# Where the second mask product of a score stage stands among the score products

## The chip, the cores and the metric

The kernel runs on one core of a Trainium2 chip. The metric is device time in microseconds (us) of one execution; lower is better.

## The reference

Two independent parts read the same `x` of 2048 rows by 640 and are mixed by a gate `g` per row. Part B is a gated feed-forward layer. Part A is attention in 64 segments of 32 rows, with a memory of 8 rows that is carried from one segment to the next, so that the segments form a chain. All data are bfloat16.

```python
def _A_ref(x, mem0, Wq, Wk, Wv, Wo, seg_len):      # H = 32 heads, Dh = 192, M = 8, seg_len = 32
    idx = jnp.arange(M + seg_len)
    mask = (idx[:, None] < M) | (idx[:, None] >= idx[None, :])
    mem = mem0
    for s in range(n_seg):
        h = jnp.concatenate([mem, x[:, s * seg_len:(s + 1) * seg_len, :]], axis=1)
        q, k, v = (jnp.einsum('btd,dhe->bhte', h, W) for W in (Wq, Wk, Wv))
        scores = jnp.einsum('bhqe,bhke->bhqk', q, k) * scale
        scores = jnp.where(mask[None, None], scores, -1000000000.0)
        o = jnp.einsum('bhqk,bhke->bhqe', _softmax(scores), v)
        o = jnp.einsum('bhte,hed->btd', o, Wo)
        mem = o[:, :M, :]
        outs.append(o[:, M:, :])
    return jnp.concatenate(outs, axis=1)
...
return g * a + (1 - g) * b       # g = sigmoid(sum(x * gate_w)), a = part A, b = part B
```

## The kernel before, in words

Part B and the left columns of the first segments are worked out in the first stretch. Then `segment(s)` runs 64 times and issues its work in an order that is written out by hand: four lists, `PROG`, `PROG1`, `PROG` and `PROG3`, one for each `s % 4`. Each item of a list is one piece of work: `("g", group, k)` is a step of the projections Q, K and V (`proj`), `("tq", o)` and `("tk", o)` transpose the rows of Q and K (`row_transp`), `("sc", o)` makes the scores, `("ex", o)` the softmax, `("pt", o)` transposes the probabilities (`p_transp`), `("pv", o)` multiplies by V (`pv_oct`) and `("wo", ...)` projects out (`wo_part`, `wo_both`). The 32 heads go in four octets of eight, `o` from 0 to 3 (`NOCT` is 4).

TensorE's array is used in column tiles. The projections (L1138, L226, L930) and the output products (L1338, L1364) write 32 output rows each, four side by side; the probabilities' transposes (L1249, L1254) do so too. Scores and `pv_oct` (L1282, L1284) use two halves of 64 columns, at tile positions `(0, 0)` and `(0, 64)`, below called the lower and the upper half.

`scores(s, o)` fills one bank of PSUM with the scores of eight heads, four in each half, 40 by 40 each (`R` is 40: 32 rows and 8 of memory). The heads have 192 values, that is one and a half chunks of 128, so each head's score is one "outer" product over a whole chunk (L1195) and one "inner" product over half a chunk (L234 by `_matmul_rows` for the lower half; L1202 for the upper one, over a copy `Qz` of Q with zeros). Before them one product by the identity writes the mask into 4 x 40 columns of each half (L1187): with `start=True` it overwrites, and the score products add to it. The two masks are one operation of the scheduler, the sixteen score products are the next. Its inputs come from DVE (the transposes into `Qs` and `Ks`) and POOL (`Qz`, L1179, and the left columns, `left_fill`, L1012). After it DVE takes the row maximum (L1214).

The scheduler `_Sched` records operations, each a list of instructions on one engine, and derives from what they read and write which semaphores each must wait for. `finalize` drops waits that are already implied. `emit_stream` issues each remaining wait by `wait_ge` (L203) ahead of the operation's first instruction; where there is more than one, all but one become instructions of their own (EVENT_SEMAPHORE in the trace). For TensorE `finalize` first tries to hang waits on the last instructions of the operation in front:

```python
if E == "pe" and len(waits) > 1 and op.idx > 0:
    prev = self.streams["pe"][op.idx - 1]
    ...
    room = 0 if prev.name.startswith("ffn") else len(prev.fns) - 1 - len(prev.tail_waits)
    ...
        if room > 0 and sn.get("pe", -1) < prev.idx:
            moved.append(wv)
            room -= 1
        else:
            keep.append(wv)
```

Of the kernel before, what the change touches and what calls it, by code (L numbers as in the profile page):

```python
# [231 lines left out]
def _matmul_rows(e, out, lhsT, rhs, start, stop, tile_position):  # L232
    nm = e.bass.get_next_instruction_name()
    return e.add_instruction(mybir.InstMatmult(  # L234
        name=nm, start_tensor_calc=start, stop_tensor_calc=stop, tile_size=(128, 64), tile_position=tile_position,
        bass_skip_group_check=True, ins=[e.lower_ap(rhs), e.lower_ap(lhsT)], outs=[e.lower_ap(out)]))


def _build(nc, A_x, A_mem0, A_Wq, A_Wk, A_Wv, A_Wo, seg_len, w_gate, w_up, w_down,
# [13 lines left out]
    NOCT = NT // 4  # L253
# [4 lines left out]
    R = L + M  # L258
# [15 lines left out]
    S_ = _Sched(nc)  # L274
# [62 lines left out]
    ps = nc.alloc_psum_tensor("ps", [128, 8, 512], F32)  # L337
# [3 lines left out]
    o = wsA_base - wsB_total  # L341
# [6 lines left out]
    o = wsA_base  # L348
# [4 lines left out]
    o = ffn_base  # L353
# [66 lines left out]
    SC = 512 - 4 * R  # L420
# [37 lines left out]
    o = ffn_base - sum(fp_sz.values())  # L458
# [5 lines left out]
    gp = [fview(fp_off["gr"] + 4 * NSEG * i, 4 * NSEG) for i in range(4)]  # L464
# [38 lines left out]
    r_ps = [Rg("ps", b, b + 1) for b in range(8)]  # L503
# [96 lines left out]
    o = 0  # L600
# [73 lines left out]
    def load_residents(cls, pick=lambda key: True):  # L674
        for key in first:
# [7 lines left out]
           reads=[r_ident], writes=[r_ident])  # L683
# [10 lines left out]
    for i in range(2):  # L694
# [3 lines left out]
               reads=[r_elw], writes=[r_elw])  # L698
# [18 lines left out]
    for h in range(NH):  # L717
        for w_, sb_, rw_, nm in ((w_gate, wg_sb, r_wg, "wg"), (w_up, wu_sb, r_wu, "wu")):
            S_.add("sp", lambda e, h=h, w_=w_, sb_=sb_: e.dma_start(
                sb_[h], w_.rearrange("(p k) f -> p k f", p=128)[:, :, FH * h:FH * (h + 1)]),  # L720
                writes=[rw_[h]], dma_sem="%s%d" % (nm, h))
# [255 lines left out]
    for n, (g, o) in enumerate(units):  # L977
# [7 lines left out]
        if g == 0:  # L985
            S_.add("pool", lambda e, o=o, b=b: e.tensor_copy(out=stg[o // 2][:, o % 2], in_=lst[b][:, 0]), reads=[r_lst[b]], writes=[r_stgh[o // 2][o % 2]],
                   name="stg s0 o%d" % o)
# [22 lines left out]
    def left_fill(s, i):  # L1010
        o, h = octet(s, i), i // 2
        S_.add("pool", lambda e: e.tensor_copy(out=Qs[:, :, L:R], in_=stg[h][:, o % 2, 0]), reads=[r_stgh[h][o % 2]], writes=[r_Ql],  # L1012
               name="Ql s%d o%d" % (s, o))
        S_.add("pool", lambda e: e.tensor_copy(out=Ks[:, :, L:R], in_=stg[h][:, o % 2, 1]), reads=[r_stgh[h][o % 2]], writes=[r_Kl],
               name="Kl s%d o%d" % (s, o))
# [166 lines left out]

    def scores(s, o):
        bank = 5 + o % 2
        fns = []
        for gp in (0, 64):
            fns.append(lambda e, gp=gp: e.matmul(  # L1187
                ps[gp:gp + R, bank, SC:512].rearrange("p (t r) -> p t r", r=R),
                ident[:, 0:R], maskm.rearrange("p (o r) -> p o r", o=1).broadcast_to([128, 4, R]),
                start=True, stop=False, tile_position=(0, gp), skip_group_check=True))  # L1190
        S_.add("pe", fns, reads=[r_ident, r_maskm], writes=[r_ps[bank]], name="mask s%d o%d" % (s, o))
        fns = []
        for tl in range(4):
            for gp, c in ((0, 3 * tl), (64, 3 * tl + 2)):
                fns.append(lambda e, gp=gp, c=c, tl=tl: e.matmul(  # L1195
                    ps[gp:gp + R, bank, SC + tl * R:SC + (tl + 1) * R], Qs[:, c, :], Ks[:, c, :], start=False, stop=False,
                    tile_position=(0, gp), skip_group_check=True))
        for tl in range(4):
            c = 3 * tl + 1
            fns.append(lambda e, c=c, tl=tl: _matmul_rows(  # L1200
                e, ps[0:R, bank, SC + tl * R:SC + (tl + 1) * R], Qs[0:64, c, :], Ks[0:64, c, :], False, True, (0, 0)))
            fns.append(lambda e, c=c, tl=tl: e.matmul(  # L1202
                ps[64:64 + R, bank, SC + tl * R:SC + (tl + 1) * R], Qz[:, tl, :], Ks[:, c, :], start=False, stop=True,
                tile_position=(0, 64), skip_group_check=True))
        S_.add("pe", fns, reads=[r_Qm, r_Ql, r_Qz, r_Km, r_Kl], writes=[r_ps[bank]],
               name="sc s%d o%d" % (s, o))
        if o + 1 < NOCT:
            left_fill(s, o + 1)
        S3 = ps[0:104, bank, SC:512].rearrange("p (t r) -> p t r", r=R)
        mxs = st_f[o % 2][0][0:104, :]  # L1210
        rst = r_st[o % 2]
        mxb = mxs.rearrange("p (t o) -> p t o", o=1).broadcast_to([104, 4, R])
        rb = r_ps[bank]
        S_.add("dve", lambda e: e.tensor_reduce(out=mxs, in_=S3, axis=AX.X, op=ALU.max),  # L1214
               reads=[rb], writes=[rst], name="smax max")
        S_.add("dve", lambda e: e.tensor_tensor(out=S3, in0=S3, in1=mxb, op=ALU.subtract),  # L1216
               reads=[rb, rst], writes=[rb], name="smax sub")
# [244 lines left out]
    def segment(s):  # L1462
# [3 lines left out]
        for n, item in enumerate(PROGS[q]):  # L1466
# [12 lines left out]
            elif kind == "tk":  # L1479
                row_transp(s, 1, i)  # L1480
            elif kind == "sc":
                scores(s, i)
            elif kind == "ex":
                softmax(s, i)
# [192 lines left out]
```

## Time and profile before

| | |
|---|---|
| timed runs | 1657.43, 1655.54, 1647.93 us; median 1655.54 |
| span of the profiled execution | 2114.2 us; the page gives it no other time |
| granted TensorE clock in it | 0.654 |
| TensorE (PE) busy | 2098.0 us, 99% of the span |
| mask products, L1187 | 512, mean 247 ns |
| outer score products, L1195 | 2048, mean 180 ns |
| waits of their own on TensorE's loader, L203 | 54, median 51 ns |

The span is that of one execution under the profiler, at its granted clock; the timed runs are other executions. In the rows of the trace PE is a product, PEld the load of its weights, and the q of PEldq stands for the sequencer in front of an engine. Starts are us from the begin of the span. The duration of a product contains the depth of the pipe, so products overlap, and the pace is read from starts. A merged row shows the start of its first instruction and the end of its last.

### The profile page before, as it was taken

What the parts mean: (1) busy time and instruction counts of PE and PEld (TensorE: products, weight loads), DVE (VectorE), ACT (ScalarE), POOL (GpSimd) and SP (SyncE); (2) the same over time, 40 slices, a digit from 0 to 9 for tenths busy, and PEclk for the clock granted to TensorE, in tenths of its full rate; (3) what the DMA queues carried; (4) which work ended last, traced back from release to release, by engine and by line L of the source; (5) the groups of instructions that cost most, each with busy time, mean ns of one, the idle gap of its engine ahead of it and who ended that gap; (6) DMA issues with size and microseconds to landing.
All of it is one profiled execution on the core that took longest, in us unless ns stands there. A gap on an engine that the chain in (4) does not pass through costs nothing.

```text
span 2114.2 us, 75845 instructions
## 1 busy us (share of the span) xinstructions
PE 2098.0 (99%) x37107; PEld 958.1 (45%) x28147; DVE 1005.8 (48%) x3039; ACT 792.9 (38%) x1890; POOL 553.3 (26%) x1625
## 2 busy tenths in 40 slices
PE   9999999999999999999999999999999999999997
PEld 3444344444444444444444444444444444444444
DVE  4233254554545454545545454545455454545453
ACT  1111244343434343444434343434444343434342
POOL 1000023232232223232222323232322223222332
PEclk6666666666666666666666666666666666666666
DMA  9612577776768777677767677776777676777775
GB/s 319 182 33 57 184 268 260 248 270 232 253 219 275 244 258 241 227 255 254 274 233 249 221 268 249 255 251 225 248 256 270 239 258 212 261 256 249 254 264 174
DMA packets 275415, 499.28 MB, mean 236 GB/s; under 512 B 121119, under 2 KB 136327, under 8 KB 275079
## 3 DMA queue, kind: packets, MB, share of 16 engines
q1 hardware_dynamic: 271000, 491.30, 68.8%
q8 instruction: 255, 4.18, 0.8%
q10 hardware_dynamic: 4079, 3.14, 0.5%
q14 instruction: 81, 0.66, 0.1%
HBM read 473.25 MB, written 21.09 MB: 234 GB/s over the span
## 4 chain that ended last, share of the span: by engine, by line
PE 99%; DMA 0%; DVE 0%; SPq 0%; POOL 0%; ACT 0%; issue 0%; ACTq 0%; POOLq 0%; DVEq 0%
PE ps L226 26%; PE ps L1138 25%; PE ps L1338 9%; PE ps L1383 8%; PE ps L1282 4%; PE ps L930 4%; PE ps L839 4%; PE ps L836 4%; PE ps L862 3%; PE ps L1364 3%; PE ps L1187 2%; PE ps L1284 2%; PE ps L234 1%; PE ps L1195 1%; PE ps L971 1%; PE ps L1254 1%
## 5 line engine op out<-in xcount | busy, mean ns | idle before, releaser
L226 PE MATMUL ps<-arena 128*32 128x384 bf16 x8960 | 887.8, 430 | 0.4 <-ACT arena L1159 0.4
L1138 PE MATMUL ps<-arena 128*32 128x384 bf16 x8640 | 857.5, 420 | 2.0 <-DVE arena L1583 2.0
L1138 PEld LDWEIGHTS ps<-arena 128*32 128x32 bf16 x8640 | 303.3, 117 | 525.3 <-issue 379.7
L1176 DVE STREAM_TRANSPOSE arena<-arena 128x384 bf16<-128x384 bf16 x512 | 276.5, 562 | 144.1 <-ACT arena L1159 144.1
L1159 ACT ACTIVATE arena<-ps 128x384 bf16<-128x384 f32 x512 | 230.0, 491 | 160.1 <-PE ps L1138 160.1
L1214 DVE TENSOR_REDUCE arena<-ps 104x4 f32<-104x160 f32 x256 | 83.0, 324 | 340.2 <-PE ps L1202 340.2
L1338 PE MATMUL ps<-arena 128*32 128x320 bf16 x3456 | 241.0, 404 | 0.0
L1012 POOL COPY arena<-arena 128x96 bf16<-128x96 bf16 x256 | 70.2, 274 | 475.3 <-PE ps L1202 311.4
L1267 ACT ACTIVATE arena<-ps 128x448 bf16<-128x448 f32 x192 | 104.4, 544 | 237.7 <-PE ps L1254 233.3
L1179 POOL COPY arena<-arena 64x160 bf16<-64x160 bf16 x256 | 81.9, 320 | 385.5 <-DVE arena L1176 384.3
L1162 ACT ACTIVATE arena<-ps 128x384 bf16<-128x384 f32 x256 | 125.2, 489 | 128.1 <-PE ps L1138 127.5
L1383 PE MATMUL ps<-arena 128*64 128x320 bf16 x1536 | 169.6, 387 | 0.0
L1226 ACT ACTIVATE ps<-ps 104x160 f32<-104x160 f32 x256 | 74.8, 292 | 239.5 <-DVE ps L1216 239.5
L1320 ACT ACTIVATE arena<-ps 128x480 bf16<-128x480 f32 x192 | 109.5, 570 | 93.8 <-PE ps L1284 85.7
L930 PE MATMUL ps<-arena 128*32 128x384 bf16 x1280 | 142.5, 408 | 0.0
L1338 PEld LDWEIGHTS ps<-arena 128*32 128x32 bf16 x3456 | 113.3, 129 | 56.9 <-ACT arena L1261 18.1
L1282 PE MATMUL ps<-arena 128*64 128x160 bf16 x1536 | 135.2, 263 | 0.0
L1284 PE MATMUL ps<-arena 128*64 128x64 bf16 x1536 | 128.6, 225 | 0.0
L1228 DVE TENSOR_REDUCE arena<-ps 104x4 f32<-104x160 f32 x256 | 81.8, 319 | 88.4 <-ACT ps L1226 87.4
L1383 PEld LDWEIGHTS ps<-arena 128*64 128x64 bf16 x1536 | 93.2, 127 | 49.4 <-issue 9.6
L1282 PEld LDWEIGHTS ps<-arena 128*64 128x64 bf16 x1536 | 94.1, 126 | 42.8 <-ACT arena L1159 23.0
L1411 ACT ACTIVATE arena<-ps 128x384 bf16<-128x384 f32 x120 | 57.3, 491 | 123.9 <-DVE arena L1580 74.0
(102 smaller groups left out, 2518.2 us busy)
## 6 DMA issues: line engine op xcount, KB each, us to landing
arena<-in_A_Wk_dram SPq DMA_DIRECT2D x335, 384.0 KB, 5.8
arena<-in_A_Wv_dram SPq DMA_DIRECT2D x335, 384.0 KB, 8.4
arena<-in_A_Wo_dram SPq DMA_DIRECT2D x205, 480.0 KB, 4.3
arena<-in_A_Wq_dram SPq DMA_DIRECT2D x209, 384.0 KB, 4.8
arena<-left_qk_scratch SPq DMA_DIRECT2D x126, 96.0 KB, 3.9
left_qk_scratch<-arena SPq DMA_DIRECT2D x49, 192.0 KB, 4.6
left_qk_scratch<-arena SPq DMA_DIRECT2D x30, 96.0 KB, 3.7
ffn_b_scratch<-arena ACTq DMA_DIRECT2D x16, 160.0 KB, 2.3
```

Source lines behind the costliest of these rows:

```text
L226: return e.add_instruction(mybir.InstMatmult(name=nm, start_tensor_calc=like["start"], stop_tensor_calc=stop, tile_size=(128, 32), tile_po ...
L930: fns.append(lambda e, outp=outp, rhs=rhs, j=j: e.matmul(outp, lhs, rhs, start=(k == 0), stop=(k == KT - 1), tile_position=(0, 32 * j)))
L1138: fns.append(lambda e, outp=outp, rhs=rhs, j=j: e.matmul(outp, lhs, rhs, start=(k == 0), stop=(k == KT - 1), tile_position=(0, 32 * j)))
L1159: S_.add("act", lambda e, m=m, bk=bk: e.activation(out=rows_sb[m], in_=ps[:, bk, 0:384], func=ACTF.Copy), reads=[r_ps[bk]], writes=[r_rows ...
L1162: S_.add("act", lambda e, i=i, bk=bk: e.activation(out=v_sb[i % NVB].rearrange("p (c n) -> p c n", c=3), in_=ps[:, bk, 0:384].rearrange("p ...
L1176: S_.add("dve", lambda e: e.transpose(out=dst[:, :, 0:L], in_=rows_sb[m].rearrange("p (c r) -> p c r", r=L)), reads=[r_rows[m]], writes=[r ...
L1267: S_.add("act", lambda e: e.activation(out=PT, in_=ps[:, bank, 0:PTW + 128], func=ACTF.Copy), reads=[r_ps[bank]], writes=[r_PT], name="pT ...
L1282: return [lambda e: e.matmul(full, v[:, e0:e0 + 64], PTm[:, i], start=True, stop=False, tile_position=(0, 64 * i), skip_group_check=True), ...
L1284: lambda e: e.matmul(part, vl[:, e0:e0 + 64], PTl[:, i], start=False, stop=True, tile_position=(0, 64 * i), skip_group_check=True)]
L1320: S_.add("act", lambda e: e.activation(out=apx(u[:, 0, 0, :], [[rs, na], [3 * rs, 4], [1, R]]), in_=ps[:, A, 0:na * W].rearrange("p (c t r ...
L1338: fns.append(lambda e, i=i, t=t, j=j, gv=gv: e.matmul(ps[32 * j:32 * j + 32, bank, 0:2 * DJ].rearrange("p (h n) -> p h n", h=2), lhs2[i], ...
L1383: S_.add("pe", [lambda e, i=i, g_=g_, c=c, p=p, u=u: e.matmul(ps[64 * i:64 * i + 64, LB, 0:2 * DJ], u[:, c, :], g_[:, c, 2 * DJ * i:2 * DJ ...
```

## The change

In octets 0 to 2 the mask operation holds only the lower half's mask. The score operation then issues four upper outer products (the first with `start=True`), four pairs of a lower outer and an upper inner product, the upper half's mask (adding, `start=False`), and the four lower inner products. In the last octet (`early`) the instructions and their order are those of before. All products and their sizes are the same.

```diff
     def scores(s, o):
         bank = 5 + o % 2
-        fns = []
-        for gp in (0, 64):
-            fns.append(lambda e, gp=gp: e.matmul(
+        early = o == NOCT - 1
+
+        def mask_mm(gp, start):
+            return lambda e: e.matmul(
                 ps[gp:gp + R, bank, SC:512].rearrange("p (t r) -> p t r", r=R),
                 ident[:, 0:R], maskm.rearrange("p (o r) -> p o r", o=1).broadcast_to([128, 4, R]),
-                start=True, stop=False, tile_position=(0, gp), skip_group_check=True))
-        S_.add("pe", fns, reads=[r_ident, r_maskm], writes=[r_ps[bank]], name="mask s%d o%d" % (s, o))
-        fns = []
-        for tl in range(4):
-            for gp, c in ((0, 3 * tl), (64, 3 * tl + 2)):
-                fns.append(lambda e, gp=gp, c=c, tl=tl: e.matmul(
-                    ps[gp:gp + R, bank, SC + tl * R:SC + (tl + 1) * R], Qs[:, c, :], Ks[:, c, :], start=False, stop=False,
-                    tile_position=(0, gp), skip_group_check=True))
-        for tl in range(4):
+                start=start, stop=False, tile_position=(0, gp), skip_group_check=True)
+
+        S_.add("pe", [mask_mm(gp, True) for gp in ((0, 64) if early else (0,))], reads=[r_ident, r_maskm], writes=[r_ps[bank]],
+               name="mask s%d o%d" % (s, o))
+
+        def outer(gp, c, tl, start=False):
+            return lambda e: e.matmul(
+                ps[gp:gp + R, bank, SC + tl * R:SC + (tl + 1) * R], Qs[:, c, :], Ks[:, c, :], start=start, stop=False,
+                tile_position=(0, gp), skip_group_check=True)
+
+        def inner(gp, tl):
             c = 3 * tl + 1
...
+        low = [outer(0, 3 * tl, tl) for tl in range(4)] + [inner(0, tl) for tl in range(4)]
+        high = [outer(64, 3 * tl + 2, tl, not early and tl == 0) for tl in range(4)] + [inner(64, tl) for tl in range(4)]
+        if early:
+            fns = [x for y in zip(low, high) for x in y]
+        else:
+            fns = high[:4] + [x for y in zip(low[:4], high[4:]) for x in y] + [mask_mm(64, False)] + low[4:]
+        S_.add("pe", fns, reads=[r_Qm, r_Ql, r_Qz, r_Km, r_Kl] + ([] if early else [r_ident, r_maskm]), writes=[r_ps[bank]],
                name="sc s%d o%d" % (s, o))
```

More of the change, by code (lines that the diff above doesn't have):

```diff
@@ L1199, in scores @@
+        def outer(gp, c, tl, start=False):
[3 more added lines that the diff above has]
+        def inner(gp, tl):
             c = 3 * tl + 1
-            fns.append(lambda e, c=c, tl=tl: _matmul_rows(
-                e, ps[0:R, bank, SC + tl * R:SC + (tl + 1) * R], Qs[0:64, c, :], Ks[0:64, c, :], False, True, (0, 0)))
@@ L1202, in scores @@
-            fns.append(lambda e, c=c, tl=tl: e.matmul(
+            if gp == 0:
+                return lambda e: _matmul_rows(
+                    e, ps[0:R, bank, SC + tl * R:SC + (tl + 1) * R], Qs[0:64, c, :], Ks[0:64, c, :], False, True, (0, 0))
+            return lambda e: e.matmul(
                 ps[64:64 + R, bank, SC + tl * R:SC + (tl + 1) * R], Qz[:, tl, :], Ks[:, c, :], start=False, stop=True,
-                tile_position=(0, 64), skip_group_check=True))
-        S_.add("pe", fns, reads=[r_Qm, r_Ql, r_Qz, r_Km, r_Kl], writes=[r_ps[bank]],
+                tile_position=(0, 64), skip_group_check=True)
```

## The prediction

> **What bounds the kernel now.** I read the clock first, then the busy shares and the chain of waits, then the two lines that the edit moves, then one score stage in order of time.
>
> ```profile
> core 0: 2114.2 us, clock 0.654
> ```
> ```profile
> PE 2098.0 (99%) x37107; PEld 958.1 (45%) x28147; DVE 1005.8 (48%) x3039; ACT 792.9 (38%) x1890; POOL 553.3 (26%) x1625
> ...
> PE ps L226 26%; PE ps L1138 25%; PE ps L1338 9%; PE ps L1383 8%; PE ps L1282 4%; PE ps L930 4%; PE ps L839 4%; PE ps L836 4%; PE ps L862 3%; PE ps L1364 3%; PE ps L1187 2%; PE ps L1284 2%; PE ps L234 1%; PE ps L1195 1%; PE ps L971 1%; PE ps L1254 1%
> ```
> ```profile
> L1187 PE MATMUL ps<-arena x512: 246/247/248, 258.7 to 2092.5; 128*40 128x160 bf16 x171
> its engine sat idle before it (us, times) until:
>   issue: 136.8, 208
> ```
> ```profile
> L1195 PE MATMUL ps<-arena x2048: 179/179/183, 258.8 to 2092.7; 128*40 128x40 bf16 x187
> its engine sat idle before it (us, times) until:
> who waited for it (us, times):
> ```
>
> TensorE is busy 99% of the span and the whole chain lies on it, so whatever a score stage gains or loses on TensorE goes straight into the time. The mask products (L1187) are 2% of the chain and the score products (L1195, L234, L1202) 1% or less each: what can be won is small. The last two fences say the second thing that matters: in all 512 mask and 2048 outer products nothing is ever waited for by name. The 136.8 us "issue" lie on the weight loader alone. So the semaphores of Q and K are always up in time; the mask does not cover a late transpose.
>
> **The span and the timed median.** The profiled execution was granted 0.654 of the clock and took 2114.2 us; the timed runs have a median of 1655.54, so they ran at a higher clock. What the edit touches is short products and sequencer work. In the stage below the short products follow each other at an even pace, and the clock's pauses do not show in it. I therefore work out the change in microseconds, add it to the span and, unscaled, to the median.
>
> **The stage today**, in order of time on TensorE:
>
> ```profile
> 1018.33 0.20 PE L1249 MATMUL ps<-arena 104*32 104x80 bf16 x4
> 1018.37 0.22 PE L1254 MATMUL ps<-arena 104*32 104x128 bf16 x4
> 1018.52 0.25 PE L1187 MATMUL ps<-arena 128*40 128x160 bf16 x2
> 1018.60 0.26 PE L1195 MATMUL ps<-arena 128*40 128x40 bf16 x8
> 1018.71 0.18 PE L234 MATMUL ps<-arena 64*40 64x40 bf16 x1
> 1018.71 0.18 PE L1202 MATMUL ps<-arena 128*40 128x40 bf16 x1
> 1018.73 0.18 PE L234 MATMUL ps<-arena 64*40 64x40 bf16 x1
> 1018.73 0.18 PE L1202 MATMUL ps<-arena 128*40 128x40 bf16 x1
> 1018.76 0.18 PE L234 MATMUL ps<-arena 64*40 64x40 bf16 x1
> 1018.76 0.18 PE L1202 MATMUL ps<-arena 128*40 128x40 bf16 x1
> 1018.78 0.18 PE L234 MATMUL ps<-arena 64*40 64x40 bf16 x1
> 1018.78 0.18 PE L1202 MATMUL ps<-arena 128*40 128x40 bf16 x1
> 1018.89 0.41 PE L1138 MATMUL ps<-arena 128*32 128x384 bf16 x2
> ```
>
> Read the starts; the durations contain the pipe's latency. Two masks start together and occupy both halves for 0.08 us (18.52 to 18.60). Then come eight pairs, a lower and an upper product starting together, at 0.025 us a pair (18.60 to 18.78 is seven steps, 0.18). From the last start to the next 32-wide group it takes 0.11 us. Mask to next: 0.37 us.
>
> Where a 64-wide operation follows, there is no such change of tile width and the last step is short:
>
> ```profile
> 1002.14 0.18 PE L1202 MATMUL ps<-arena 128*40 128x40 bf16 x1
> 1002.16 0.24 PE L1282 MATMUL ps<-arena 128*64 128x160 bf16 x2
> 1002.17 0.12 PEld L1284 LDWEIGHTS ps<-arena 128*64 128x64 bf16 x2
> 1002.24 0.19 PE L1284 MATMUL ps<-arena 128*64 128x64 bf16 x2
> ```
>
> Here it is about 0.025 us, the pace of a pair (stage: 0.29 us). The same rows give a 160-column product between others as 0.07 to 0.08 us (2.16 to 2.24).
>
> **Part 1: the moved mask.** Each half of the array holds, before and after, one mask (0.07 to 0.08) and eight short products. What changes is who is beside whom. Before, mask beside mask (0.08), then eight pairs (0.20): 0.28. After, the lower mask beside four upper products, four pairs, then the upper mask beside four lower products. If 0.025 us is the price of a product in its own half, the upper half alone is 8 x 0.025 + 0.08 = 0.28 again: nothing is won. If it were the price of two products sharing one path, the four beside a mask would hide under it: 0.08 + 0.10 + 0.08 = 0.26, a gain of 0.02. The first two rows of the stage decide for me: L1249 starts four products with four weight loads, and 0.04 us later the next four start. Four loads and four 80-column streams in 0.04 us mean that the shared path passes an instruction in 0.01 us or less, so 0.025 us for a pair is not the shared path; it belongs to one half. [...] I take 0 for this part; ends -0.03 (all but the mask hides) and +0.015 (the 0.10 against 0.08, with the end drained a little later).
>
> **Part 2: where the waits go.** The score operation waits for two semaphores: DVE (transposes of Q and K) and POOL (Qz, and the left columns). An instruction carries one. Today the scheduler hangs the first on the last instruction of the operation in front, the mask, if that has more than one: its room is `len(prev.fns) - 1`. The mask operation has two instructions, room 1. The edit leaves it one, room 0. So in three octets of each segment both waits stand on the first score product, and one becomes an instruction of its own on TensorE's queue: 3 x 64 = 192 more. The trace has such instructions, 54 of them, none near a score stage:
>
> ```profile
> L203 PEldq EVENT_SEMAPHORE  x54: 51/51/94, 6.3 to 2106.7; - x54
> ```
>
> It takes 51 ns. Is it hidden? Two rows about where one starts, two about what follows:
>
> ```profile
> 1178.17 0.12 PEld L1383 LDWEIGHTS ps<-arena 128*64 128x64 bf16 x2
> ```
> ```profile
> L203 PEldq EVENT_SEMAPHORE  x1: 51/51/51, 1178.2 to 1178.2; - x1
> ```
> ```profile
> L203 PEldq EVENT_SEMAPHORE  x1: 51/51/51, 2046.2 to 2046.2; - x1
> ```
> ```profile
> 2046.28 0.22 PEld L1364 LDWEIGHTS ps<-arena 128*32 128x32 bf16 x12 [0.61 <-ACT arena L1310]
> ```
>
> At 1178 the wait stands right behind a weight load: it is reached once the load in front has started, not far ahead of it. Nothing suffers there, since 320-column products are still streaming. At 2046 nothing is streaming: from the wait (2046.2) to the next load (2046.28) it is about 0.08 us, though part of that may be ACT, which the row names. In a score stage the load in front is that of the lower mask, and it starts only when the array has drained for the change of width. So the wait begins with the mask, and behind it in TensorE's queue stands every other product of the stage, those that were to run beside the mask first. The first upper product then starts 0.05 us (the instruction alone) to 0.10 us (0.08 and a late entry) after the mask; I take 0.08, the exposed row. The mask's 0.08 us then cover nothing.
>
> **The sum for one stage.** Upper half: 0.08, then eight products 0.20, then the upper mask at 0.28. Beside it the four lower inner products, the last starting 0.075 later, at 0.355. Then 0.11 to a 32-wide successor: 0.465 against 0.37 to 0.375. With a 64-wide successor: 0.38 against 0.29. Both: +0.09 us. Bounds, from 0.05 and 0.10: +0.06 to +0.115.
>
> For 192 stages: 192 x 0.09 = **17.3 us** (11.5 to 22). Profiled span: 2131.5. Median: 1655.5 + 17.3 = **1672.8**, own range 1667 to 1678. About 0.5%, 8.3 us or 43 ns a stage, is what a measurement of this kernel can tell from no change.
>
> What else moves: the softmax maximum and the POOL copies of the next left columns start 0.09 us later; I cost them at nothing, because TensorE hardly waits for anyone. The two largest rows of its waits in the whole trace are one single event and three short ones:
>
> ```profile
> PE ps L1202 <- POOL arena L1296: 6.3, 1, 6.3
> PE ps L1138 <- DVE arena L1583: 2.0, 3, 0.7
> ```
>
> So the engines behind the scores have slack; if that cover were gone, a late octet would add its 0.09 us once more. No DMA is moved, the last octet is left as it is, and the number of products is the same.
>
> **The rivals.**
>
> *The wait is hidden.* If the sequencer gets through it while the mask's load still waits for the drain, only part 1 is left: 0 to +0.015 us a stage, at most 192 x 0.015 = 2.9 us: 1655.5 to 1658.4. For it: the 51 ns are shorter than the drain. Against: the row at 1178.
>
> *Not slower: short products hide under the mask.* The wait is hidden and the 0.025 us belong to the pair. Then 0.02 to 0.03 us a stage go: 3.8 to 5.8 us, 1650 to 1652. It turns the sign only if the first upper product starts within 0.03 us of the mask. The row of 51 ns speaks against it, and so does L1249's step.
>
> *Strict order.* Products might have to end in program order. A 40-column product (179 ns) beside a mask (247 ns) may then not finish first and starts 0.07 us later. Behind the lower mask the wait hides that; behind the upper mask the four lower products start 0.07 later, and a stage costs 0.09 + 0.07 = 0.16 us more: 31 us, 1686. [...] The trace speaks against it:
>
> ```profile
> 1007.21 1.35 PE L1364 MATMUL ps<-arena 128*32 128x160 bf16 x46
> 1008.39 0.40 PE L930 MATMUL ps<-arena 128*32 128x384 bf16 x3
> 1008.40 0.37 PE L1364 MATMUL ps<-arena 128*32 128x160 bf16 x2
> ```
>
> Two products of L1364, all of which stand earlier in the program, start after three of L930: columns of the array run ahead of one another.
>
> **How the numbers follow.** Forecast 0.52, hidden wait 0.27, hiding under the mask 0.11, strict order 0.10. The forecast's low end touches the 0.5% line, and timed runs spread over 9 us: slower by over 0.5% gets 0.47 from the forecast, 0.02 from the second case, 0.10 from the fourth, together 0.59; within 0.5% 0.05 + 0.23 + 0.04 = 0.32; faster 0.02 + 0.07 = 0.09. The range, 1652 to 1685, holds the forecast and the hidden wait and leaves out most of the last two.
>
> **What would show it.** In the changed profile: 54 + 192 = 246 waits of their own on TensorE's loader; the first upper product about 0.08 us behind the lower mask; then four upper products alone, at 0.025; the stage 0.46 us long before a 32-wide successor. The first upper product within 0.02 us of the mask would show the wait hidden; a step under 0.02 beside the mask would show part 1 wrong; lower products starting 0.07 after the upper mask would show strict order.

## The result: slower by about 1.4%, and the profile after

The changed kernel has a median of 1674.89 us (1668.08 to 1680.14, four runs) against 1651.74 us of the kernel before in the same comparison: a ratio of 1.0145, interval 1.010 to 1.019, which is 16.5 to 31 us and in the middle 23 us. A second comparison on another occasion gave 1.0100 [1.0069, 1.0130], 15.9 us between the medians. The forecast was +17.3 us.

The profile of before that the prediction read was taken at a granted clock of 0.654. The profile of after was granted 0.995, so it is compared here with a second profile of the kernel before, taken at 0.996 (the first experiment). First the cores view of both, after and then before:

```profile
core 0: 1678.4 us, clock 0.995
```
```profile
core 0: 1650.9 us, clock 0.996
```

The page of after (busy time, then the chain that ended last by engine), and the same two rows of before at this clock:

```profile
PE 1576.2 (94%) x37107; PEld 780.3 (46%) x28147; DVE 998.6 (59%) x3039; ACT 784.9 (47%) x1890; POOL 549.8 (33%) x1625
...
PE 75%; DVE 9%; DMA 7%; issue 4%; ACT 4%; SPq 1%; POOL 0%; DVEq 0%; ACTq 0%; POOLq 0%
```
```profile
PE 1563.7 (95%) x37090; PEld 773.6 (47%) x28147; DVE 998.7 (60%) x3039; ACT 784.5 (48%) x1890; POOL 549.5 (33%) x1625
...
PE 68%; DMA 18%; DVE 7%; ACT 4%; issue 3%; SPq 1%; POOL 0%; DVEq 0%; ACTq 0%; POOLq 0%
```

At a clock of 0.996 the kernel before isn't bound by TensorE alone: DMA has 18% of its chain and DVE 7%. So the first fact of the prediction, that the whole chain lies on TensorE, was a fact about the execution at 0.654. After, DMA's share is 7%. These are shares of one chain in one execution each, not a measure of the loss: experiment 9 below loses 0.87% and has 15%.

The waits of their own on TensorE's loader in after (columns: count, min/median/max ns, first and last start):

```profile
L203 PEldq EVENT_SEMAPHORE  x246: 51/51/93, 6.2 to 1672.2; - x123
```

These are the 54 + 192 that were forecast. No load and no product of TensorE in this trace has more than one wait: 2681 loads and 505 products have one, the others none. The next two fences show what the outer score products wait for, in before at clock 0.996 and in after. At 0.654 nothing stood under these headings. The idle times count the loads of the weights along with the products; of the products alone, those behind DVE are 3.3 us (14 times) in before and 9.0 us (29 times) in after.

```profile
L1195 PE MATMUL ps<-arena x2048: 179/179/198, 177.1 to 1629.1; 128*40 128x40 bf16 x187
its engine sat idle before it (us, times) until:
  DVE arena L1176: 8.9, 29
```
```profile
L1197 PE MATMUL ps<-arena x2048: 179/179/198, 179.1 to 1657.3; 128*40 128x40 bf16 x187
its engine sat idle before it (us, times) until:
  DVE arena L1176: 13.9, 42
  POOL arena L1179: 10.2, 28
```

**A stage whose inputs are there in time.** The timeline of TensorE in after, one stage in front of a 64-wide successor:

```profile
845.68 0.25 PE L1188 MATMUL ps<-arena 128*40 128x160 bf16 x1
845.68 0.29 PE L1197 MATMUL ps<-arena 128*40 128x40 bf16 x6
845.80 0.18 PE L1206 MATMUL ps<-arena 128*40 128x40 bf16 x1
...
845.87 0.18 PE L234 MATMUL ps<-arena 64*40 64x40 bf16 x1
...
845.89 0.18 PE L234 MATMUL ps<-arena 64*40 64x40 bf16 x1
845.90 0.23 PE L1188 MATMUL ps<-arena 128*40 128x160 bf16 x1
845.92 0.21 PE L234 MATMUL ps<-arena 64*40 64x40 bf16 x2
845.97 0.24 PE L1293 MATMUL ps<-arena 128*64 128x160 bf16 x2
```

The first upper product starts with the lower mask (3 ns later in the single rows), not 0.08 us behind it, and from mask to next it is 0.29 us, the same as before. The wait that was to serialise the two stands elsewhere (the answer for L203 in this stretch):

```profile
L203 PEldq EVENT_SEMAPHORE  x1: 51/51/51, 845.2 to 845.2; - x1
```

In the single rows it starts 0.47 us ahead of the mask, while the projections in front were still streaming. There is nothing of it to see in this stage.

**A stage whose inputs are late.** Octet 1 of segment 41, before at clock 0.996, TensorE's products:

```profile
1122.63 0.44 PE L1187 MATMUL ps<-arena 128*40 128x160 bf16 x2
1122.84 0.28 PE L1195 MATMUL ps<-arena 128*40 128x40 bf16 x6
...
1123.20 0.35 PE L1138 MATMUL ps<-arena 128*32 128x384 bf16 x4
```

The second mask holds the hung wait for POOL: both masks together last 0.44 us instead of 0.25, and the first score product follows it at once. It is 0.57 us from mask to next. The same stage in after, products and then weight loads:

```profile
1141.26 0.25 PE L1188 MATMUL ps<-arena 128*40 128x160 bf16 x1
1141.59 0.26 PE L1197 MATMUL ps<-arena 128*40 128x40 bf16 x7
...
1141.79 0.23 PE L1188 MATMUL ps<-arena 128*40 128x160 bf16 x1
1141.82 0.18 PE L234 MATMUL ps<-arena 64*40 64x40 bf16 x1
1141.95 0.35 PE L1138 MATMUL ps<-arena 128*32 128x384 bf16 x4
```
```profile
1141.56 0.18 PEld L1197 LDWEIGHTS ps<-arena 128*40 128x40 bf16 x7 [0.21 <-POOL arena L1179]
```
```profile
L203 PEldq EVENT_SEMAPHORE  x1: 51/51/51, 1141.5 to 1141.5; - x1
```

Here the wait instruction, which waits for DVE, starts long after the mask. In the single rows DVE's transpose (L1176) ends at 1141.444, and POOL's copy, which the load's row names because the load itself waits for it, at 1141.435. The wait runs from 1141.485 to 1141.536, only then comes the first load, at 1141.562, and the first score product starts at 1141.593: 0.149 us behind the transpose. In before, where this wait rides on the load, it is 0.055 us (1122.783 to 1122.838). The upper mask costs nothing here: in before it too came only after the waiting, and from the first score product to the next group it is 0.36 us in both. It is 0.69 us from mask to next instead of 0.57.

Read from the single rows of the trace, all 192 stages of octets 0 to 2 fall into such classes. In after 81 of the 192 wait instructions start behind the mask and 111 ahead of it; the median of all is 0.18 us ahead. The late stages are octet 0 of the segments with `s % 4` of 0, 1 and 2, and octet 1 of those with 1 and 2: 80 of the 192. In before their first score product starts 0.11 to 0.47 us behind the masks in the medians, in all the others 0.083. Median from mask to next, in ns (sixteen stages each):

| stages | before, clock 0.996 | after |
|---|---|---|
| octet 0, s % 4 = 0 / 1 / 2 (late) | 487 / 471 / 471 | 578 / 565 / 567 |
| octet 1, s % 4 = 1 / 2 (late) | 567 / 824 | 622 / 946 |
| octet 0, s % 4 = 3 (in time) | 375 | 381 |
| octet 1, s % 4 = 0 (in time) | 375 | 382 |
| octet 2, s % 4 = 0 (in time) | 287 | 290 |

So a late stage loses 0.055 to 0.12 us and a stage that is in time loses 0 to 0.007; the classes left out of the table differ by 4 ns at most. The sum over octets 0 to 2 is 90.0 us in before and 99.1 in after: 9 us, nearly all of it in the late stages (45.6 and 54.6). In all five late classes the step is the one of this example: from the end of DVE's transposes to the first score product it is 0.055 us in before and 0.148 in after, 0.09 more, and from there to the next group 0.36 in both (medians). Summed over the 80 late stages 7.0 us of the growth lie between the transposes' end and the first product. The rest of the loss isn't in these stages, and experiment 6 will show that a longer stage need not be time lost.

**The rest: stalls without a named cause.** The waits of TensorE by line (us in total, times, longest), first of before at 0.996, then of after:

```profile
PE ps L1364 <- DMA arena<-in_A_Wo_dram: 7.4, 17, 0.9
...
PE ps L1364 <- issue: 6.2, 9, 1.5
PE ps L1338 <- issue: 5.3, 11, 0.8
...
PE ps L1138 <- issue: 1.9, 2, 1.4
```
```profile
PE ps L1375 <- issue: 10.9, 12, 1.8
PE ps L1349 <- issue: 10.7, 14, 1.4
...
PE ps L1138 <- issue: 8.1, 13, 1.1
PE ps L1375 <- DMA arena<-in_A_Wo_dram: 4.0, 7, 0.9
```

"issue" is idle time in which the engine waited for nothing that the profile shows. L1338 and L1364 of before are L1349 and L1375 of after. They grew from 11.5 to 21.6 us, on output products that the edit doesn't touch, and L1138 from 1.9 to 8.1. In part they may replace waits for weights: those for the output weights fell from 7.4 to 4.0 us, those of L1138 for the weights of V from 6.3 to 1.2. Idle stretches of over 0.4 us on TensorE with no wait on the instruction that ends them, counted from 250 us on: 21 with 15.3 us in before, 44 with 37.8 us in after.

### The profile page after: what moved, and what is told of

Read it like the earlier page. It is cut to its first block, busy times and chain, and to the rows that moved or that the text cites. A ratio compares the mean times of both kernels' runs of the same rounds, so it can differ in the third digit from the quotient of the medians.

```text
span 1678.4 us, 76037 instructions
## 1 busy us (share of the span) xinstructions
PE 1576.2 (94%) x37107; PEld 780.3 (46%) x28147; DVE 998.6 (59%) x3039; ACT 784.9 (47%) x1890; POOL 549.8 (33%) x1625
## 4 chain that ended last, share of the span: by engine, by line
PE 75%; DVE 9%; DMA 7%; issue 4%; ACT 4%; SPq 1%; POOL 0%; DVEq 0%; ACTq 0%; POOLq 0%
PE ps L1138 19%; PE ps L226 18%; PE ps L1394 7%; PE ps L1349 6%; PE ps L1293 3%; DMA arena<-in_A_Wo_dram 3%; PE ps L839 3%; PE ps L836 3%; PE ps L930 3%; PE ps L1375 2%; PE ps L1197 2%; PE ps L862 2%; PE ps L1188 2%; DVE arena L1176 2%; DMA arena<-in_A_Wk_dram 1%
## 5 line engine op out<-in xcount | busy, mean ns | idle before, releaser
L1138 PE MATMUL ps<-arena 128*32 128x384 bf16 x8640 | 644.2, 328 | 15.7 <-issue 8.1
L226 PE MATMUL ps<-arena 128*32 128x384 bf16 x8960 | 649.1, 326 | 5.9 <-issue 2.0
L1138 PEld LDWEIGHTS ps<-arena 128*32 128x32 bf16 x8640 | 229.4, 96 | 388.7 <-issue 272.2
L1176 DVE STREAM_TRANSPOSE arena<-arena 128x384 bf16<-128x384 bf16 x512 | 272.9, 558 | 68.3 <-ACT arena L1159 67.0
L1349 PE MATMUL ps<-arena 128*32 128x320 bf16 x3456 | 185.7, 300 | 14.3 <-issue 10.7
L1012 POOL COPY arena<-arena 128x96 bf16<-128x96 bf16 x256 | 69.8, 273 | 269.1 <-PE ps L234 159.5
L1394 PE MATMUL ps<-arena 128*64 128x320 bf16 x1536 | 122.7, 304 | 3.2 <-issue 3.0
L1293 PE MATMUL ps<-arena 128*64 128x160 bf16 x1536 | 117.8, 240 | 6.9 <-issue 3.6
L1349 PEld LDWEIGHTS ps<-arena 128*32 128x32 bf16 x3456 | 91.2, 96 | 57.8 <-ACT arena L1272 17.5
L930 PE MATMUL ps<-arena 128*32 128x384 bf16 x1280 | 111.3, 328 | 1.5 <-issue 1.5
L1188 PE MATMUL ps<-arena 128*40 128x160 bf16 x512 | 110.4, 240 | 0.6
L1339 POOL COPY arena<-arena 128x96 bf16<-128x96 bf16 x192 | 51.3, 267 | 168.5 <-ACT arena L1321 104.1
L1295 PE MATMUL ps<-arena 128*64 128x64 bf16 x1536 | 104.2, 193 | 1.9 <-issue 1.9
```

The source lines that it names most:

```text
L226: return e.add_instruction(mybir.InstMatmult(name=nm, start_tensor_calc=like["start"], stop_tensor_calc=stop, tile_size=(128, 32), tile_po ...
L930: fns.append(lambda e, outp=outp, rhs=rhs, j=j: e.matmul(outp, lhs, rhs, start=(k == 0), stop=(k == KT - 1), tile_position=(0, 32 * j)))
L1138: fns.append(lambda e, outp=outp, rhs=rhs, j=j: e.matmul(outp, lhs, rhs, start=(k == 0), stop=(k == KT - 1), tile_position=(0, 32 * j)))
L1176: S_.add("dve", lambda e: e.transpose(out=dst[:, :, 0:L], in_=rows_sb[m].rearrange("p (c r) -> p c r", r=L)), reads=[r_rows[m]], writes=[r ...
L1188: return lambda e: e.matmul(ps[gp:gp + R, bank, SC:512].rearrange("p (t r) -> p t r", r=R), ident[:, 0:R], maskm.rearrange("p (o r) -> p o ...
L1293: return [lambda e: e.matmul(full, v[:, e0:e0 + 64], PTm[:, i], start=True, stop=False, tile_position=(0, 64 * i), skip_group_check=True), ...
```

## The experiments

Intervals are 95%. Six to twelve runs stand behind each changed kernel's median and 17 to 23 behind that of the kernel before beside it; the first experiment is one run.

**1. The kernel before, once more**, for a profile at the full clock. No edit.

> The kernel before, unchanged, for a profile at whatever clock this chip grants. Theory A (inputs come late once the clock is high): at a granted clock near 1 some score stages show the first outer product more than 0.1 us behind the masks, up to 0.2 us, in about half of the octets 0 to 2, and the stages add up to well over the 94 us of the throttled profile. Theory B (the prediction's: a wait of its own begins with the mask, in every stage): the stages look as in the throttled profile, first outer product 0.08 us behind the masks in all of them.

One run, 1652.66 us, span 1650.9. Its rows are shown above. It shows that at this clock inputs of the scores do come late.

**2. The wait alone.** The kernel before with its order of products; only the scheduler's room behind a mask is taken away in octets 0 to 2, so that both waits stand on the score operation.

```diff
-room = 0 if prev.name.startswith("ffn") else len(prev.fns) - 1 - len(prev.tail_waits)
+room = 0 if prev.name.startswith("ffn") or (prev.name.startswith("mask") and not prev.name.endswith("o3")) else ...
```

> The kernel before with one thing changed: in octets 0 to 2 no wait is hung on the mask operation, so DVE's wait is an instruction of its own, 192 more; the products and their order are those of before. Theory A: the wait is reached early and costs nothing where inputs are early; where they are late it adds 0.04 to 0.06 us, in some 100 stages: 4 to 6 us, ratio 1.003 to 1.004. Theory B: 0.05 to 0.08 us behind the masks, which last 0.08 us: hidden, ratio 1.000 to 1.002. Theory C (the order of the products costs): 1.000.

1666.76 us against 1652.49: 1.0094 [1.0070, 1.0119]. Its late stages lose 0.04 to 0.09 us in the medians: the first score product starts 0.147 us behind the transposes, as in after, and what follows is 0.05 us shorter than in before (0.306 against 0.36), since the upper mask, which no longer waits for POOL, runs while TensorE waits anyway. The sum of octets 0 to 2 is 95.3 us, 5.3 more than before. These are the 4 to 6 us of theory A, but 14.3 us are lost: none of the three theories gave this much. Its longest stall is this one, TensorE's timeline and, behind it, the queues of data and of instructions in a stretch ahead of the stall's end (queue, kind, packets, MB, share):

```profile
1407.09 0.33 PE L1138 MATMUL ps<-arena 128*32 128x384 bf16 x3
1410.16 0.32 PE L1138 MATMUL ps<-arena 128*32 128x384 bf16 x1 [2.74 <-issue]
```
```profile
q1 hardware_dynamic: 187, 0.52, 98.6%
q8 instruction: 1, 0.02, 4.4%
```

Three products of a step that has four run, and the fourth comes 2.74 us later though its row names nothing that holds it. The queues are those of 1407.2 to 1408.5 us: one packet on the instruction queue, from 1407.63 to 1408.55 in the single rows, and TensorE goes on 1.6 us after its end.

**3. The order alone.** Both masks in front, the waits hung as before, the score products in the order of the change.

```diff
+S_.add("pe", [mask_mm(gp, True) for gp in (0, 64)], ...)
...
+fns = high[:4] + [x for y in zip(low[:4], high[4:]) for x in y] + low[4:]
```

> Both masks in front as before, with both waits hung as before; in octets 0 to 2 the score products in the order of the change (four upper outer, four pairs of lower outer and upper inner, four lower inner). Theory A and B: the halves are separate queues of equal length, 0 to 2 us, ratio 0.999 to 1.002. Theory C: the four upper products run alone and so do the four lower ones, 0.1 to 0.2 us a stage: 19 us or more, ratio 1.011 or more.

1651.65 us: 1.0013 [0.9992, 1.0033]. The order costs nothing that can be measured.

**4. The upper mask behind the waits, old order.** It is the first product of the score operation.

```diff
+fns = ([] if early else [mask_mm(64, True)]) + [x for y in zip(low, high) for x in y]
```

> The order of before, but in octets 0 to 2 the upper half's mask is the first product of the score operation, behind both waits, and DVE's wait is an instruction of its own. Theory A: in the late stages the upper mask, 0.07 to 0.08 us, no longer lies under the wait for the inputs: some 100 x 0.08 = 8 us, and the wait of its own on top, 4 to 6 us: ratio 1.007 to 1.009. Theory B: 0.08 us in each of 192 stages, 15 us, ratio 1.009, with early stages longer too. Theory C: 1.000 to 1.003.

1666.55 us: 1.0091 [1.0065, 1.0117], the same as the wait alone. Theories A and B both had about 1.009 and aren't told apart by the time. Its stages are longer than those of the wait alone (98.8 against 95.3 us in octets 0 to 2), since in a late stage the upper mask no longer runs while TensorE waits anyway; in the time this doesn't show.

**5. A wait that holds nothing up.** The kernel before, its waits hung as before, and in octets 0 to 2 one more wait in front of the scores, for a semaphore value reached at the start of the program.

```diff
             eng.wait_ge(s, v)
+        if eng_name == "pe" and op.name.startswith("sc ") and not op.name.endswith("o3"):
+            eng.wait_ge(self.sems["act"], 1)
```

> The kernel before, its waits hung as before, and in octets 0 to 2 one more wait on the score operation, for a value of ACT's semaphore that was reached at the start of the program: 192 more instructions of the same kind as in the change, none of which ever holds the queue up. Theory F (a wait of its own whose semaphore is not yet up holds TensorE's sequencer, so that it falls back behind the fetch of its instructions; stalls without a named cause follow): 0 to 3 us, ratio 1.000 to 1.002, some 20 stalls over 0.4 us without a named cause, as in the kernel before. Theory G (the instruction itself costs, wherever it stands): as the wait alone, 14 us, ratio 1.009.

1666.08 us against 1652.15: 1.0079 [1.0047, 1.0111]. The instruction costs about as much when it waits for nothing, which rules out theory F. Its stages are only 2.7 us longer than before in octets 0 to 2; but it has 36 unnamed stalls of over 0.4 us with 29.8 us, against 21 with 15.3.

**6. The change without an instruction of its own.** The lower mask is cut into two products of 80 columns, so that the operation has two instructions and the wait hangs on the second.

```diff
-[mask_mm(gp, True) for gp in ((0, 64) if early else (0,))]
+[mask_mm(gp, True) for gp in (0, 64)] if early else [mask_mm(0, True, 0, 2), mask_mm(0, False, 2, 2)]
```

> The change, with the lower half's mask cut into two products of 80 columns, so that the mask operation has room for a wait again and no wait is an instruction of its own. Theory F and G alike: the waits of their own and what they bring are gone; what is left is the upper mask behind the inputs where these are late, some 80 stages x 0.07 to 0.08 us = 6 us, and 192 short products: ratio 1.002 to 1.006, some 20 stalls over 0.4 us. If the ratio stays at 1.012 or more, it is the place of the upper mask that costs, not the wait.

1654.16 us: 1.0017 [0.9998, 1.0036]. The changed kernel's order and its split masks, without the 192 instructions, can't be told from the kernel before. Yet its stages of octets 0 to 2 are 6.6 us longer (96.6 us), about the 6 us that were expected to be lost; 2.0 us were, with an interval from -0.3 to 5.9. In the profile the waits of TensorE that the view puts down to DMA (over 0.15 us, from 250 us on) are 8.0 us in place of 13.9. In the late stages the first product starts 0.055 us behind the transposes in the median, as in before; the late stages are 5.0 us longer in all, 3.1 of them behind the first product. So a longer stage isn't time lost by the kernel one for one.

```profile
L203 PEldq EVENT_SEMAPHORE  x54: 51/51/94, 6.1 to 1644.0; - x54
```

**7. The same with the old wait of experiment 5.**

> As the change without own waits, and in octets 0 to 2 the wait on the long reached value of ACT's semaphore as an instruction of its own. Theory F: as without it, ratio 1.002 to 1.006. Theory G: 1.011 to 1.015.

1671.75 us: 1.0115 [1.0090, 1.0140]. Put back as an instruction that waits for nothing, it brings the loss back.

**8. The change again**, in the same comparison as 5, 6 and 7.

> The change itself on the same chip as the three others: ratio 1.010 to 1.019 by the first comparison, and about 40 stalls over 0.4 us without a named cause.

1668.05 us: 1.0100 [1.0069, 1.0130].

**9. The old wait in octet 0 alone:** 64 instructions instead of 192.

```diff
+        if eng_name == "pe" and op.name.startswith("sc ") and op.name.endswith("o0"):
+            eng.wait_ge(self.sems["act"], 1)
```

> As the old wait alone, but in octet 0 only: 64 more wait instructions, none of which holds the queue up. Theory G (0.07 us each, wherever it stands): 4 to 5 us, ratio 1.002 to 1.004. Theory H (only short products behind it are hit, since they eat up the sequencer's lead): the same, 1.002 to 1.004.

```profile
L205 PEldq EVENT_SEMAPHORE  x64: 51/51/51, 178.3 to 1640.4; - x64
```

1666.57 us against 1650.77: 1.0087 [1.0053, 1.0121]. A third of the instructions, about the whole loss, where both theories had 1.002 to 1.004: it isn't so much per instruction. The stages of octets 0 to 2 are 0.7 us longer than in before; nearly everything is lost elsewhere.

**10 and 11. The old wait ahead of the projections:** in front of step 1 of V (192 instructions), and of Q, K and V (576), in octets 0 to 2. Two waits are written, since one of them rides on the next product.

```diff
+        if eng_name == "pe" and op.name[:3] == "V s" and op.name[-5:] in ("o0 k1", "o1 k1", "o2 k1"):
+            eng.wait_ge(self.sems["act"], 1)
+            eng.wait_ge(self.sems["dve"], 1)
```

> 192 wait instructions on long reached values, none at a score stage: ahead of the second step of V's projection in three octets of each segment, where 384-column products run before and behind. Theory G: 13 to 15 us, ratio 1.007 to 1.010, with some 35 stalls over 0.4 us without a named cause. Theory H: 0 to 5 us, ratio 1.000 to 1.003, and some 20 such stalls.

> 576 wait instructions on long reached values, ahead of the second step of Q's, K's and V's projections in three octets of each segment. Theory G: three times the 192, 40 to 45 us, ratio 1.023 to 1.028. Theory H: 0 to 10 us, ratio 1.000 to 1.006. If the stalls have a limit, the ratio lies between, at 1.010 to 1.018.

```profile
L206 PEldq EVENT_SEMAPHORE  x576: 51/51/51, 173.1 to 1643.5; - x192
```

1655.29 and 1655.30 us against 1650.77: 1.0025 [1.0003, 1.0046] and 1.0028 [1.0002, 1.0053]. Three times the instructions cost no more, and 576 of them here cost a third of what 64 cost at the scores. The place matters, the number hardly.

**12. Three more products instead of a wait:** in each mask operation of octets 0 to 2 one more product of eight columns that adds zeros, with the weights kept; 192 more instructions, none of them a wait. It tests whether the loss comes from shifting what stands where in the instruction stream.

```diff
+if o < NOCT - 1:
+    fns.append(lambda e: _matmul_kept64(e, ps[0:R, bank, SC + XA:SC + L], ident[:, 0:R], maskm[:, XA:L]))
```

> The kernel before, its waits hung as before, and in octets 0 to 2 one more product behind the masks: eight columns of the lower half's mask that are zero, added once more with the identity still loaded. It adds as many instructions at the same places as the change does (192), so that the fetch of TensorE's instructions falls on the same places of the program, and no wait of its own. Theory I (it is the wait instruction): at most 192 x 0.025 = 4.8 us where the product shows, ratio 1.000 to 1.003, some 20 stalls over 0.4 us. Theory J (any added instruction moves the fetch to worse places): 1.007 to 1.010, some 35 stalls.

1651.25 us against 1653.05: 0.9982 [0.9958, 1.0006]. So many instructions more cost nothing. No version was shown to beat the kernel before.

**Where the idle time goes.** All idle stretches of TensorE over 0.15 us from 250 us on, counted in the trace of each kernel's profiled execution, without the one of about 8 us near the end, which each of them has in front of a score product that waits for POOL; "named" is where the instruction that ends one has a wait:

| kernel | span, us | unnamed, us | named, us | sum | waits of their own at the scores |
|---|---|---|---|---|---|
| 3 order alone | 1648.9 | 17.6 | 29.6 | 47.2 | 0 |
| 6 change, no own wait | 1650.2 | 19.0 | 27.9 | 46.9 | 0 |
| 1 before again | 1650.9 | 18.3 | 30.8 | 49.1 | 0 |
| 10 old wait, V | 1652.3 | 21.1 | 32.0 | 53.1 | 0 (192 elsewhere) |
| 11 old wait, Q K V | 1654.1 | 31.7 | 23.2 | 54.9 | 0 (576 elsewhere) |
| 4 late mask | 1658.8 | 27.7 | 24.9 | 52.6 | 192 |
| 12 more products | 1661.6 | 25.3 | 32.5 | 57.8 | 0 |
| 5 old wait | 1664.0 | 33.2 | 25.7 | 58.9 | 192 |
| 2 wait alone | 1665.9 | 33.9 | 27.3 | 61.2 | 192 |
| 8 change again | 1666.2 | 32.3 | 24.5 | 56.8 | 192 |
| 7 old wait in 6 | 1672.3 | 34.7 | 26.1 | 60.8 | 192 |
| 9 old wait, octet 0 | 1672.4 | 34.9 | 31.7 | 66.6 | 64 |
| after | 1678.4 | 41.1 | 24.4 | 65.5 | 192 |

The unnamed part is 27.7 us or more in every kernel with waits of their own at the scores, and 25.3 or less in the others but one: the 576 waits at the projections, which have 31.7 us but 7.6 us less named waiting than before. The sum follows the span over the table, though not line by line; the profiled execution of 12 was the slowest of its twelve, and the median of their times lies 12 us below its own; that of after was the slowest of its four. Each row is one execution.

**What these unnamed stalls are.** Counting TensorE's loads, products and waits in order of time, every unnamed stall of over 0.4 us in every kernel of the table ends at an instruction with the same place modulo 256 (176 or 177 in some traces, 193 or 194 in those that hold 17 more records of products): they all lie at boundaries of blocks of 256 instructions. The queue view of before and of after (packets, MB):

```profile
q8 instruction: 255, 4.18, 1.0%
```
```profile
q8 instruction: 256, 4.19, 1.0%
```

Each packet has 16384 bytes (single rows of after). TensorE's loads, products and waits of their own are 65291 records in before and 65500 in after, 255.0 and 255.9 times 256: one packet for each block, and worked out from these numbers 64 bytes for each instruction. By the single rows a block takes TensorE 5.9 us in the median and about 4 us at the fastest, and the packet of the next block, counted in order, starts 2.2 to 2.6 us after the boundary before it in the median; and every one of these stalls ends 1.15 to 1.7 us after a packet has landed. So, as I read it, a stall comes where a block runs through faster than the next packet comes, and both sides count: in after the blocks that end in such a stall run for 5.18 us without it, the others for 5.95 (medians), and their packets start 3.6 us behind the boundary, those of the others 2.1. The latest packet starts 4.2 to 4.7 us behind the boundary in before, 3, 6, 10, 11 and 12, and 5.2 to 6.8 us in all the kernels with waits of their own at the scores.

The packets come while the data queues are at work. Where these keep the DMA engines over 80% busy in the first 4 us of a block, the packet starts 2.6 us behind the boundary in the median in before and 3.0 in after; where they are less than half busy, 1.2 in both. All packets that are later than 4 us fall where they are 84% busy or more (counted in before, 2, 3, 9 and after). Whether the packets queue behind the weights wasn't tested by itself.

What stays open is why a wait at the score stage delays some of these packets and one at the projections hardly. That the instruction costs is shown by adding it (2, 5, 7, 9) and by taking it away (6). That the cost runs by way of these packets is seen in the traces that go with it, and wasn't tested by itself.

## Why the prediction was right, and where not

**Sign and size came out, and the instruction that causes the loss; the way by which it does so did not.** +17.3 us was forecast, in its own range of 11.5 to 22; 23 us (16.5 to 31) and 15.9 us were measured. The cause named, a wait that finds no room on a mask operation of one instruction, is confirmed from both sides: the wait without the order gives 1.0094, the order without the wait 1.0013, the whole change without the wait 1.0017. The 54 + 192 waits of 51 ns are in the trace.

**Part 1 at zero was right.** In a stage that is in time the last product starts 0.263 us after the mask, where it was 0.265 (medians). The 0.10 against 0.08 in the range of this part is four of my steps of 0.025 against one mask; no run shows it as a loss. In 104 stages of after, those whose first upper product starts within 0.03 us of the mask, the four upper products start 0.003, 0.046, 0.071 and 0.096 us behind the mask, the next upper one at 0.121, the first lower one at 0.083 (medians), and the stage is no longer for it. That the short steps don't go with the clock held: from pair to pair of outer products it is 25 to 29 ns in all 256 stages at 0.654, while a group of 384-column products took 0.233 us to the next in the median, against 0.163 at 0.995. Experiments 3 and 6 put order and split at +0.13 and +0.17%, both with 1 inside the interval, whose upper ends are 0.33 and 0.36%.

**Part 2 came near in total, and that is luck.** Three of its steps failed:

*"So the wait begins with the mask."* I carried the row at 1178, a wait right behind a weight load, over to all stages. That the mask's load starts late behind products of another width is in the trace: in before at 0.654 it starts 0.145 to 0.400 us behind the start of the last product in front, 71 to 73 ns ahead of that product's modelled end in all 256 stages. That the array is empty by then isn't shown; that was my estimate. But the wait need not stand behind this load: in after 111 of 192 waits start ahead of the mask and are hidden. For these the rival "the wait is hidden" was right, 0 to 0.007 us a stage where it said 0 to 0.015.

*"So the semaphores of Q and K are always up in time."* That held at a clock of 0.654, where TensorE was busy for 99% of the span and none of the 2048 outer products waited for an engine by name. At 0.995 80 stages are late. There an exposed wait has its place: 0.055 to 0.12 us more a stage, with 0.09 in the middle, but for another reason than I gave: the instruction stands behind the arriving semaphore and moves the first score product from 0.055 to 0.148 us behind DVE's transposes, 0.09 us, near the 0.08 of the exposed row that I took. The place of the upper mask adds nothing, since in before it waited as well. The product 192 x 0.09 should have been 80 x 0.09: 7 of the 9 us by which the stages of octets 0 to 2 grew. I had noted that the span's clock differed from that of the timed runs, and carried over the stage's waits all the same.

*A missing term.* The unnamed stalls, which but for 2.5 us in after lie outside these stages, grew from 18.3 to 41.1 us, by 22.8 us, where 23 us were lost. No step of mine had them: they carry the name "issue" in the view of waits, and I read that heading only at the mask. Experiment 9 loses 15.8 us with stages only 0.7 us longer; experiment 6 has stages 6.6 us longer and no loss that can be measured. So how much of the 9 us of the stages reaches the time is open, and it may be little: while they grew, the waits put down to DMA fell from 13.9 to 4.6 us. The total fits because a term that I had much too large stands where one is missing that I didn't know.

**The other rivals.** Short products hiding under the mask: not seen, 0.263 against 0.265 us. Strict order: the four lower products were to start 0.07 us behind the upper mask, which starts at 845.90; two of them start ahead of it (845.87, 845.89) and two at 845.92, though all four stand behind it in the program. So starts don't keep the order of the program between the halves here; the ends are modelled and can't show theirs, and no run shows the 0.07 us. The rivals that would not be slower are excluded by the interval.

**The cover.** That "the engines behind the scores have slack" can't be judged from these runs apart from the rest: DVE's share of the chain went from 7% to 9%. DMA is a cover that I hadn't seen: by the waits put down to it (13.9 us in before, 8.0 in 6, 4.6 in after) part of what TensorE loses in the stages it would have spent waiting for weights. This was read from one execution each and not tested.

## What to carry to other kernels

Before an operation is cut down to one instruction, look which waits were riding on its last ones: a wait that becomes an instruction of its own can cost more than the work that was moved, even when its semaphore was reached long ago (1.0079 in experiment 5, where the order alone in 3 had 1.0013). That a stage has become longer is not yet time lost: experiments 6 and 9 had the one without the other. The profile at a clock of 0.654 showed the work but none of the waits for DVE at the outer products, that at 0.996 showed 29 of them; what is late and what is in time must be read at the clock of the timed runs. And read the "issue" rows as well as the named waits: in after they held 37.8 us of stalls of over 0.4 us, all of which end at the boundary of a block of 256 instructions, 1.15 us or more after a packet of the instruction queue has landed.

## What was not expected of the hardware

- TensorE's instructions came in packets of 16 KB, 256 packets to 65500 instructions in after; a packet started later where the data queues kept the DMA engines busy (3.0 us behind the boundary over 80%, 1.2 below half, in after). In before 21 unnamed stalls of over 0.4 us (15.3 us in all), all of them at such a boundary, are 0.9% of the span; in after it is 44 and 37.8 us, 2.3%. The longest seen is 2.74 us.
- The price of one wait of 51 ns depended on where it stood: 64 at the first octet's scores cost 0.87% (14 to 16 us, over 200 ns for each), 576 ahead of projection steps 0.28% (about 8 ns for each).
- The sequencer took such a wait ahead of the products in front of it (in after 0.18 us ahead of the mask in the median, one in ten over 0.40), so its 51 ns vanished in a stage whose inputs were up: 0 to 0.007 us longer. Where the inputs were late the same instruction cost more than its 51 ns: the first product started 0.148 us behind DVE's transposes instead of 0.055.
